# Turned attention weights in rows of 2304 bytes, turned behind the masks, with the values two steps later

## The chip, the cores and the metric

The kernel runs on one core of a Trainium2 chip. The metric is the device time of one execution in microseconds (us), the median of several runs. Engines are named as in the profile: PE is TensorE's matmuls (PEld its weight loads), DVE is VectorE, ACT is ScalarE, POOL is GpSimd, SP is SyncE, which here only issues DMAs; SPq, ACTq and so on are the sequencers of the engines.

## The reference

Attention with a threshold on 8 x 8 heads of 576 positions and 64 dimensions, then an MLP with a squared relu on the 4608 tokens that the heads give, all in float32.

```python
scores = scale * np.matmul(q, k.transpose(0, 1, 3, 2))
thresh = np.max(scores, axis=-1, keepdims=True) - tau
scores = np.where(scores >= thresh, scores, -1000000000.0)
attn = exp(scores - max);  attn = attn / (sum(attn) + 1e-09)
x = matmul(attn, v)            # (B,H,S,D) -> (B*S, H*D) = (4608, 512)
h = x @ w_in                   # 512 -> 2048
return np.maximum(h, 0.0) ** 2 @ w_out
```

## The kernel before, in words

**Visits and steps.** Two heads make a head pair. A visit is a head pair with some of its five blocks of queries (four of 128, and the odd one, number 4, of 64). The first twelve visits fill the time in which the weights of the MLP are read; from visit 12 on, visits come in pairs of two head pairs: the first visit of a pair (even number) has the odd block, shared by the two, and blocks 0 to 3; the second (odd number) has blocks 0 to 3. A step is one block of one visit, so a pair has nine steps: the odd block, four of the first visit, four of the second. `late_step` writes out what each of these steps puts on each engine, in program order; there is no scheduler behind it, and every engine does its work in that order.

**A step.** PE makes the scores (`scores_of_two` makes those of two blocks at once, in every second step). DVE takes the maxima (L303), ACT the exponents (L318), DVE applies the threshold, which the change's title calls masks (L330), and POOL divides by the sum (L340). The weights of a block then lie with queries on the partitions. For the product with the values they must have keys on the partitions: they have to be turned.

**Turning and placing.** In the visits from 11 on this is done in two moves. `turn_blocks` (L420) has DVE transpose blocks of 32 x 32 from `w` into `turned`, a buffer with two halves that are used in turn. `place_blocks` then moves these small blocks across partitions with DMAs from SP's queue into `wT` (L432 for blocks 0 to 3, L437 and L445 for the odd block): sixteen DMAs for a pair of blocks (four quarters of queries x four quarters of keys, 32 partitions each, 72 KB) and sixteen of half the size for an odd block. `turn_last(s)` issues the turning of the step before and whatever placing is due; when each placing is due stands in `place_at`. In the earlier visits PE turns the weights and ACT copies them (L381, L388, L393) into `wT`.

**The product with the values.** `mix` (L482) multiplies `wT` by the values when all blocks of a visit are placed. It makes two groups: one reads the columns ONE (blocks 0 and 1) and the odd block (LEFT or ODD), the other TWO (blocks 2 and 3). Within each the first sixteen or so matmul records are the eight terms of the four full key blocks; the last terms, for the odd keys, follow for both. It uses the PSUM banks of areas in which scores of even steps lie, so their masks have to be done first. `mixes` says in which step it stands: `lag` steps after the visit's last block; `at_end` puts it at the end of the step for first visits, else it stands near the start.

**The MLP** fills PE between these: `fill(quarter)` takes as many pieces (`mlp_in` L530, `unit` L638, `product` L744) from a queue as an even rate asks for. A piece's follow-ups on ACT, DVE and POOL (L646, L650, L569 and others) are issued one or two pieces later by `after()` and `some_later()`.

Of the kernel before, what the change touches and what calls it, by code (L numbers as in the profile page):

```python
# [19 lines left out]
def kernel(  # L20
# [52 lines left out]

    NC9 = 2 * NBLK + 1
    ODD, ONE, LEFT, TWO = 0, REST, REST + 2 * P, 2 * REST + 2 * P
    wT = const.tile([P, NC9, S + REST], FP32, name="wT")

    vs = [const.tile([P, 2 * NBLK + 2, D], FP32, name=f"vs{i}") for i in range(2)]
    qmid = const.tile([P, P], FP32, name="qmid")
# [291 lines left out]
    def turn(vis, i, part):  # L371

        w = weights[vis, i][0]
        ps = take("mm", (6, 7)) if early() and part == 1 else take("tx", (4, 5))
        ps = ps.rearrange("p (c n) -> p c n", n=P)
        if i < NBLK:
            cols = slice(i * P, (i + 1) * P)
            for n in range(3):
                c = 3 * part + n
                nc.tensor.transpose(ps[:, n, :], w.rearrange("p u k -> p (u k)")[:, c * P:(c + 1) * P], ident)  # L380
            nc.scalar.copy(wT[:, 3 * part:3 * part + 3, cols], ps[:, 0:3, :])  # L381
        elif part < 2:
            rows = slice(part * D, (part + 1) * D)
            for c in range(NBLK):
                at = part * REST + c * P
                nc.tensor.transpose(ps[:, c, 0:D], w[rows, 0, at:at + P], ident[rows, rows])
            at = part * (NBLK + 1)
            nc.scalar.copy(wT[:, at:at + NBLK, NBLK * P:S], ps[:, :, 0:D])  # L388
        else:

            for rows, keys in ((slice(0, D), slice(S - REST, S)), (slice(D, P), slice(0, REST))):
                nc.tensor.matmul(ps[rows, 0, 0:D], w[rows, 0, keys], ident[rows, rows], start=True, stop=True)
            nc.scalar.copy(wT[:, NBLK, NBLK * P:S], ps[:, 0, 0:D])  # L393

    blocks = {}

    def turn_blocks(vis, i):

        w = weights[vis, i][0]
        two = i < NBLK
        both = two or paired(vis)
        M = KB - 2
        if not two or i % 2 == 0:
            at = len(blocks) % 2 * NB
            size = 2 * KB * (1 + two) if both else KB + 2
            blocks[vis, i // 2] = turned[:, at:at + size * 32].rearrange("p (k u q) -> p k u q", u=1 + two, q=32)  # L410
        wb = blocks[vis, i // 2]
        if both:
            odd = M if i in (2, 3) else KB
            parts = [(0, 0, M, 0), (0, M, KB, 2 * M + 2 - odd), (1, M, KB, odd), (1, 0, M, KB + 2)]
            if odd == KB:
                parts[0:2] = [(0, 0, KB, 0)]
        else:
            parts = [(0, 0, KB, 2), (0, M, KB, 0)]
        for u, k0, k1, at in parts:
            nc.vector.transpose(wb[:, at:at + k1 - k0, i % 2, :],  # L420
                                w[:, u, k0 * 32:k1 * 32].rearrange("p (k q) -> p k q", q=32))

    def place_blocks(vis, pair, which=range(4)):

        wb = blocks[vis, pair]
        for qb in which:
            rows = slice(qb * 32, qb * 32 + 32)
            for j in range(4):
                to = wT[j * 32:j * 32 + 32, :, :]
                if pair < NBLK // 2:  # L430
                    at = (ONE, TWO)[pair] + qb * 64
                    nc.sync.dma_start(out=to[:, :, at:at + 64], in_=wb[rows, j::4, :, :].rearrange("p c u q -> p c (u q)"))  # L432
                    continue
                at = LEFT + qb % 2 * 32
                if paired(vis):
                    at = at if qb < 2 else ODD + qb % 2 * 32
                    nc.sync.dma_start(out=to[:, :, at:at + 32], in_=wb[rows, j::4, 0, :])  # L437
                else:


                    first = j if qb < 2 else KB + (j - KB) % 4
                    n = len(range(first, KB if qb < 2 else 2 * KB, 4))
                    c = first // 4
                    first += 2 if qb < 2 else -KB
                    nc.sync.dma_start(out=to[:, c:c + n, at:at + 32],  # L445
                                      in_=wb[rows, first:first + 4 * n - 3:4, 0, :])

    read_to = {"x": 0}

# [29 lines left out]
    def mix(n, cols):  # L479

        def term(ps, u, c, at, rows=slice(0, P), first=False, last=False):
            nc.tensor.matmul(ps[u * D:(u + 1) * D, :], vs[n % 2][rows, u * (NBLK + 1) + c, :],  # L482
                             wT[rows, NBLK if c == NBLK else u * (NBLK + 1) + c, at:at + ps.shape[1]],
                             start=first, stop=last)

        above, below = slice(0, D), slice(D, P)
        arrived(vs[n % 2])
        if not by_dma(n):
            ps = take("tx", (4, 5))[:, 0:cols.stop - cols.start]
            for c in range(NBLK):  # L490
                for u in range(2):
                    term(ps, u, c, cols.start, first=(c == 0))
            for u, rows in enumerate((above, below)):
                term(ps, u, NBLK, cols.start, rows, last=True)
            put(n, cols.start, ps, False)
            return
        n1, n2 = 2 * P + REST, 2 * P
        at = ODD if paired(n) and n % 2 else ONE
        one, two = bank[0], bank[4]
        groups = (one[:, 0:n1], at, (above, below)), (two[:, 0:n2], TWO, (below, above))  # L500
        for ps, x, _ in groups:
            for c in range(NBLK):
                for u in range(2):
                    term(ps, u, c, x, first=(c == 0))

        for ps, x, places in groups:
            for u, rows in enumerate(places):
                term(ps, u, NBLK, x, rows, last=True)
        put(n, 0, one[:, ONE - at:ONE - at + 2 * P], True)
        left = ODD if at == ODD else LEFT - at  # L510
        put(n, NBLK * P, one[:, left:left + REST], False)
        put(n, 2 * P, two[:, 0:n2], True)
# [282 lines left out]
    def paired(n):  # L795

        return n >= 3 * HP
# [17 lines left out]
    for s, (n, i) in enumerate(steps):  # L815

        if by_dma(n):
            mixed = {visits[n][1][-1]: (0, 3 if n % 2 else 2)}
        else:
            mixed = {x: (x, 3) for x in range(NBLK + 1)}  # L820
        if i in mixed:
            first, lag = mixed[i]
            cols = slice(first * P, S if by_dma(n) else min((i + 1) * P, S))
            mixes[s + lag] = (n, cols)
            g_ = visits[n][0]
            if g_ % HP == HP - 1:
                complete[s + lag] = g_ // HP * S + cols.stop
# [107 lines left out]
    for s, (n, i) in enumerate(steps):  # L935
# [3 lines left out]
        more = nxt < len(visits)  # L939
        if paired(n):  # L940

            a, b = (1, 2) if paired(n - 1) else (3, 3)
            place_at[s + a].append((n, 2, (0, 1)))
            place_at[s + b].append((n, 2, (2, 3)))
            place_at[s + 3].append((n, 0))
            place_at[s + 5].append((n, 1))
            place_at[s + 7].append((n + 1, 0))
            place_at[s + 9].append((n + 1, 1))
            prep_at[s].append(lambda n=n: prep_part(q, n))
            load_at[s].append(lambda n=n: load_part(q, n + 1))  # L950
            load_at[s + 2].append(lambda n=n: load_v(n))
            prep_at[s + 4].append(lambda n=n: prep_part(q, n + 1))
            load_at[s + 4].append(lambda n=n: load_v(n + 1))
        else:
            place_at[s + 3].append((n, 0))
            place_at[s + 4].append((n, 1))
            place_at[s + 5].append((n, 2))
# [34 lines left out]
    def late_step(s):  # L992
# [3 lines left out]
        if on:  # L996
            n, i = steps[s]
            if not odd:
                scores_of_two(s)
                turn_last(s)  # L1000
            maxima(s, [area(u, odd) for u in range(2)])
            after()
            some_later("gpsimd")
            exponents(n, i)
# [5 lines left out]
                for j in chunk_at.get(s, ()):  # L1010
                    add_chunk(j)

        at_end = s in mixes and (mixes[s][0] % 2 == 0 or not paired(mixes[s][0]))
        if not at_end:
            values()
        if odd or not on:
            turn_last(s)
        quarter = rate(s) / 4 if s < END else 1e9
        fill(quarter)
        some_later("vector")  # L1020
        some_later("gpsimd")
        smooth = at_end or s not in mixes
        if smooth:
            after()
        if on:
# [4 lines left out]
        if smooth:  # L1030
            fill(quarter)
            after()
            some_later("gpsimd")
        some_loads()
        some_later("vector")
        if not smooth:
# [2 lines left out]
        some_loads()  # L1039
        fill(quarter)  # L1040
        some_loads()
        if at_end:
            values()
        fill(quarter)
        some_loads()

# [144 lines left out]
```

## Time and profile before

| | us |
|---|---|
| time before, median of 3 runs | 1415.88 (1415.67 to 1416.69) |
| span of the profiled execution | 1411.2 |
| PE busy | 1326.5 (94%) |
| DVE, POOL, ACT busy | 952.6, 978.5, 581.3 |
| first placing DMA, last placing DMA issued | 243.9, 1248.4 |

A line of the page's groups reads: line, engine, operation, what it writes and reads, shapes, count | busy us, mean ns of one | idle time of the engine just before, and what ended most of it. A line of the waits reads: engine, tile and line that waited, what it waited for: us in total, times, the longest. In a timeline a line has start, length, engine, line, operation, and in brackets the idle time before it. PE's records are two to a float32 matmul.

### The profile page before, as it was taken

What the parts mean: (1) busy time and instruction counts of PE and PEld (TensorE: products, weight loads), DVE (VectorE), ACT (ScalarE), POOL (GpSimd) and SP (SyncE); (2) the same over time, 40 slices, a digit from 0 to 9 for tenths busy, and PEclk for the clock granted to TensorE, in tenths of its full rate; (3) what the DMA queues carried; (4) which work ended last, traced back from release to release, by engine and by line L of the source; (5) the groups of instructions that cost most, each with busy time, mean ns of one, the idle gap of its engine ahead of it and who ended that gap; (6) DMA issues with size and microseconds to landing.
All of it is one profiled execution on the core that took longest, in us unless ns stands there. A gap on an engine that the chain in (4) does not pass through costs nothing.

```text
span 1411.2 us, 25854 instructions
## 1 busy us (share of the span) xinstructions
PE 1326.5 (94%) x9112; PEld 1092.8 (77%) x9112; DVE 952.6 (68%) x2026; ACT 581.3 (41%) x1357; POOL 978.5 (69%) x1229
## 2 busy tenths in 40 slices
PE   7899999888979899999999999999999999999998
PEld 5676567667868787777888878787888777889997
DVE  6877776677757766676977687778877768622231
ACT  4777673214334343424352525252525243513322
POOL 3688774686776949577787788779786867552451
PEclk8999999989999999999999999999999999999999
DMA  7755431545554544554454546554655455420000
GB/s 152 160 151 139 125 71 36 86 78 103 97 107 83 115 86 88 95 103 90 87 117 84 111 81 117 95 99 91 109 102 102 83 107 92 92 49 1 16 16 16
DMA packets 406354, 128.15 MB, mean 91 GB/s; under 512 B 390064, under 2 KB 394448, under 8 KB 406224
## 3 DMA queue, kind: packets, MB, share of 16 engines
q1 hardware_dynamic: 385632, 95.10, 37.4%
q0 software_dynamic: 18288, 31.11, 8.3%
q8 instruction: 72, 1.18, 0.4%
q10 hardware_dynamic: 2304, 0.29, 0.2%
q14 instruction: 58, 0.48, 0.1%
HBM read 50.59 MB, written 9.44 MB: 43 GB/s over the span
## 4 chain that ended last, share of the span: by engine, by line
PE 62%; POOL 15%; DVE 7%; SPq 6%; issue 4%; ACT 4%; DMA 3%; ACTq 0%; DVEq 0%; POOLq 0%
PE big L638 19%; PE big L744 18%; PE big L482 9%; PE big L282 6%; SPq L432 4%; POOL w L340 3%; PE big L530 3%; PE big L266 3%; POOL g L569 3%; DVE w L330 2%; DMA wT<-turned 2%; PE big L709 2%; PE big L380 2%; DVE st L303 2%; DVE turned L420 1%
## 5 line engine op out<-in xcount | busy, mean ns | idle before, releaser
L303 DVE TENSOR_REDUCE st<-big 128x1 f32<-128x576 f32 x288 | 203.5, 745 | 121.0 <-PE big L282 87.1
L340 POOL TENSOR_SCALAR w<-w,st 128x576 f32<-128x576 f32 x269 | 235.9, 886 | 22.7 <-DVE st L333 15.2
L420 DVE STREAM_TRANSPOSE turned<-w 128x512 f32<-128x512 f32 (+2 forms) x388 | 176.5, 499 | 103.0 <-POOL w L340 88.3
L330 DVE SCALAR_TENSOR_TENSOR w<-big,st,w 128x576 f32<-128x576 f32 x269 | 208.2, 810 | 52.9 <-ACT w L318 52.7
L744 PE MATMUL big<-wo,gsum 128*128 128x256 f32 x1088 | 243.5, 381 | 0.0
L744 PEld LDWEIGHTS big<-wo,gsum 128*128 128x128 f32 x1088 | 204.7, 190 | 35.7 <-issue 8.0
L482 PE MATMUL big<-wT,vs 128*64 128x128 f32 (+7 forms) x1700 | 180.7, 371 | 35.5 <-DMA wT<-turned 13.0
L638 PE MATMUL big<-xT,w_in_sb 128*128 128x128 f32 x1536 | 191.3, 280 | 8.2 <-ACT g L663 5.1
L338 POOL TENSOR_SCALAR st<-st 128x2 f32<-128x2 f32 (+1 forms) x148 | 34.8, 235 | 234.4 <-DVE w L330 226.7
L638 PEld LDWEIGHTS big<-xT,w_in_sb 128*128 128x128 f32 x1536 | 182.3, 195 | 18.3 <-issue 8.1
L482 PEld LDWEIGHTS big<-wT,vs 128*64 128x64 f32 (+1 forms) x1700 | 101.2, 141 | 109.2 <-issue 47.1
L744 PE MATMUL big<-wo,g 128*128 128x256 f32 x816 | 184.3, 381 | 0.0
L318 ACT ACTIVATE w<-big,st 128x576 f32<-128x576 f32 x269 | 183.5, 733 | 0.0
L744 PEld LDWEIGHTS big<-wo,g 128*128 128x128 f32 x816 | 151.8, 190 | 22.7 <-issue 3.6
L315 ACT ACTIVATE st<-st 128x2 f32<-128x2 f32 (+1 forms) x148 | 30.3, 204 | 287.4 <-DVE st L303 286.4
L282 PE MATMUL big<-kT,qT 64*128 64x256 f32 (+3 forms) x768 | 114.1, 422 | 5.6 <-DVE qT L240 4.4
L650 DVE TENSOR_TENSOR g<-big,g 128x512 f32<-128x512 f32 x96 | 64.5, 677 | 69.4 <-PE big L638 64.4
L282 PEld LDWEIGHTS big<-kT,qT 64*128 64x128 f32 x768 | 87.4, 189 | 27.1 <-issue 8.5
L646 ACT ACTIVATE g<-g 128x512 f32<-128x512 f32 x96 | 60.3, 629 | 69.8 <-DVE g L650 69.6
L520 POOL TENSOR_TENSOR gsum<-g 128x512 f32<-128x512 f32 x34 | 44.5, 1310 | 60.2 <-ACT g L647 59.8
L647 ACT ACTIVATE g<-g 128x512 f32<-128x512 f32 x128 | 80.7, 630 | 4.1
L638 PE MATMUL big<-t,g 128*128 128x128 f32 x512 | 64.7, 283 | 7.2 <-POOL g L569 6.3
(114 smaller groups left out, 2141.2 us busy)
## 6 DMA issues: line engine op xcount, KB each, us to landing
wT<-turned SPq DMA_DIRECT2D x800, 72.0 KB, 2.2
wo<-in_moe_w_in_dram SPq DMA_DIRECT2D x16, 512.0 KB, 4.5
wo<-in_moe_w_out_dram SPq DMA_DIRECT2D x16, 512.0 KB, 3.7
out_dram<-osb POOLq DMA_DIRECT2D x32, 256.0 KB, 2.4
ql<-in_q_dram POOLq DMA_DIRECT2D x96, 72.0 KB, 3.0
wT<-turned SPq DMA_DIRECT2D x192, 36.0 KB, 2.1
kl<-in_k_dram POOLq DMA_DIRECT2D x88, 72.0 KB, 2.6
vs<-in_v_dram POOLq DMA_DIRECT2D x48, 128.0 KB, 3.3
```

Of the source, the lines that this page charges most:

```text
L282: nc.tensor.matmul(big[to, at + x0:at + x1], lhsT, keys[u * D:(u + 1) * D, x0:x1], start=True, stop=True)
L303: nc.vector.tensor_reduce(out=mx[:, u:u + 1], in_=sc[u], axis=AX.XY, op=ALU.max)
L318: nc.scalar.activation(out=w[:, u, :].rearrange("p (h k) -> p h k", h=2), in_=sc[u], func=AF.Exp, bias=bias[:, u:u + 1], scale=SCALE)
L330: nc.vector.scalar_tensor_tensor(out=wu, in0=sc[u], scalar=thr[:, u:u + 1], in1=wu, op0=ALU.is_ge, op1=ALU.mult, accum_out=sm[:, u:u + 1])
L340: nc.gpsimd.tensor_scalar(out=w[:, u, :], in0=w[:, u, :], scalar1=z[:, u:u + 1], scalar2=rcp[:, u:u + 1], op0=ALU.add, op1=ALU.mult)
L420: nc.vector.transpose(wb[:, at:at + k1 - k0, i % 2, :], w[:, u, k0 * 32:k1 * 32].rearrange("p (k q) -> p k q", q=32))
L482: nc.tensor.matmul(ps[u * D:(u + 1) * D, :], vs[n % 2][rows, u * (NBLK + 1) + c, :], wT[rows, NBLK if c == NBLK else u * (NBLK + 1) + c, a ...
L638: nc.tensor.matmul(to[:, f, :], factor(j, p, q, c)[:, f * P:(f + 1) * P], part[:, c, :], start=(p in "125" and f == 0 and c == 0), stop=(p ...
L646: nc.scalar.activation(out=to, in_=to if src is None else src, func=AF.Relu)
L647: nc.scalar.activation(out=to, in_=to, func=AF.Square)
L650: nc.vector.tensor_tensor(out=x, in0=to, in1=x, op=ALU.add)
L744: nc.tensor.matmul(to, left[:, f, :], wo[:, slot, f, :], start=(f == 0), stop=(f == HF - 1))
```

## The change

It has three parts, as its title says.

The layout of `wT` goes from [key chunk, query] to [group of 64 queries, key chunk, query in the group], and that of `turned` with it, so that what one placing DMA of a full pair of blocks moves in a partition is one run of 9 x 64 floats, 2304 bytes, on both sides; before it was nine runs of 256 bytes. The odd block's placing keeps its nine runs of 128 bytes. The readers of `wT` in `mix` take groups of 64 columns, each 2304 bytes after the other.

`turn_last`, with turning and placing, moves in `late_step` from behind the scores (even steps) or behind the values (odd steps) to behind the masks and the division of the step.

The values of a pair's first visit move from the end of the pair's seventh step (lag 2, `at_end`) to near the start of its ninth (lag 4); those of the second visit stay where they were, in the third step of the next pair. The placing of the second visit's first two blocks, which overwrites what the first visit's values read, moves from step 7 to step 8 (counted from 0).

```diff
-    wT = const.tile([P, NC9, S + REST], FP32, name="wT")
+    wT = const.tile([P, S // REST + 1, NC9, REST], FP32, name="wT")
...
-            blocks[vis, i // 2] = turned[:, at:at + size * 32].rearrange("p (k u q) -> p k u q", u=1 + two, q=32)
+            t = turned[:, at:at + NB]
+            blocks[vis, i // 2] = t.rearrange("p (j c u q) -> p c j u q", j=4, u=2, q=32) if two else t.rearrange("p (k q) -> p k q", q=32)
...
+            move(wb[:, 0:h, :, :], whole_[:, 0, :, :, :])
+            if i < 2:
+                move(wb[:, h, :, :].rearrange("p (u j) q -> p u j q", u=2), rest_[:, :, 0, :, :])
+            else:
+                move(wb[:, h, 2:4, :], rest_[:, 0, 0, :, :])
+                move(wb[:, h, 0:2, :], rest_[:, 1, 0, :, :])
+            move(wb[:, h + 1:, :, :], whole_[:, 1, :, :, :])
...
-                    at = (ONE, TWO)[pair] + qb * 64
-                    nc.sync.dma_start(out=to[:, :, at:at + 64], in_=wb[rows, j::4, :, :].rearrange("p c u q -> p c (u q)"))
+                    nc.sync.dma_start(out=to[:, (ONE, TWO)[pair] // REST + qb, :, :].rearrange("p c q -> p (c q)"),
+                                      in_=wb[rows, :, j, :, :].rearrange("p c u q -> p (c u q)"))
...
-                             wT[rows, NBLK if c == NBLK else u * (NBLK + 1) + c, at:at + ps.shape[1]],
+                             wT[rows, at // REST:(at + ps.shape[1]) // REST, NBLK if c == NBLK else u * (NBLK + 1) + c, :],
...
-            mixed = {visits[n][1][-1]: (0, 3 if n % 2 else 2)}
+            mixed = {visits[n][1][-1]: (0, 3 if n % 2 else 4)}
...
-            a, b = (1, 2) if paired(n - 1) else (3, 3)
+            a, b = (1, 2) if paired(n - 1) else (2, 2)
...
-            place_at[s + 7].append((n + 1, 0))
+            place_at[s + 8].append((n + 1, 0))
...
             if not odd:
                 scores_of_two(s)
-                turn_last(s)
...
-        at_end = s in mixes and (mixes[s][0] % 2 == 0 or not paired(mixes[s][0]))
-        if not at_end:
-            values()
-        if odd or not on:
-            turn_last(s)
+        values()
...
+        turn_last(s)
         some_loads()
...
-        if at_end:
-            values()
```

More of the change, by code (lines that the diff above doesn't have):

```diff
@@ L376, in turn @@
         if i < NBLK:
-            cols = slice(i * P, (i + 1) * P)
             for n in range(3):
@@ L380, in turn @@
                 nc.tensor.transpose(ps[:, n, :], w.rearrange("p u k -> p (u k)")[:, c * P:(c + 1) * P], ident)
-            nc.scalar.copy(wT[:, 3 * part:3 * part + 3, cols], ps[:, 0:3, :])
+            nc.scalar.copy(wT[:, 2 * i:2 * i + 2, 3 * part:3 * part + 3, :].rearrange("p g c q -> p c g q"),
+                           ps[:, 0:3, :].rearrange("p c (g q) -> p c g q", g=2))
         elif part < 2:
@@ L387, in turn @@
             at = part * (NBLK + 1)
-            nc.scalar.copy(wT[:, at:at + NBLK, NBLK * P:S], ps[:, :, 0:D])
+            nc.scalar.copy(wT[:, 2 * NBLK, at:at + NBLK, :], ps[:, :, 0:D])
         else:
@@ L392, in turn @@
                 nc.tensor.matmul(ps[rows, 0, 0:D], w[rows, 0, keys], ident[rows, rows], start=True, stop=True)
-            nc.scalar.copy(wT[:, NBLK, NBLK * P:S], ps[:, 0, 0:D])
+            nc.scalar.copy(wT[:, 2 * NBLK, NBLK, :], ps[:, 0, 0:D])
     blocks = {}
@@ L404, in turn_blocks @@
         two = i < NBLK
-        both = two or paired(vis)
         M = KB - 2
@@ L408, in turn_blocks @@
             at = len(blocks) % 2 * NB
-            size = 2 * KB * (1 + two) if both else KB + 2
-            blocks[vis, i // 2] = turned[:, at:at + size * 32].rearrange("p (k u q) -> p k u q", u=1 + two, q=32)
+            t = turned[:, at:at + NB]
+            blocks[vis, i // 2] = t.rearrange("p (j c u q) -> p c j u q", j=4, u=2, q=32) if two else t.rearrange("p (k q) -> p k q", q=32)
         wb = blocks[vis, i // 2]
[L412 to L418, printed above, removed]
+        move = nc.vector.transpose
+        if two:
+            wb = wb[:, :, :, i % 2, :]
+            whole_, rest_ = (w[:, :, x0 * 32:x1 * 32].rearrange("p u (c j q) -> p u c j q", q=32, j=n)
+                             for x0, x1, n in ((0, M, 4), (M, KB, 2)))
+            h = M // 4
+            move(wb[:, 0:h, :, :], whole_[:, 0, :, :, :])
[5 more added lines that the diff above has]
+            move(wb[:, h + 1:, :, :], whole_[:, 1, :, :, :])
+            return
+        parts = [(0, 0, KB, 0), (1, M, KB, KB), (1, 0, M, KB + 2)] if paired(vis) else [(0, 0, KB, 2), (0, M, KB, 0)]
         for u, k0, k1, at in parts:
-            nc.vector.transpose(wb[:, at:at + k1 - k0, i % 2, :],
-                                w[:, u, k0 * 32:k1 * 32].rearrange("p (k q) -> p k q", q=32))
+            move(wb[:, at:at + k1 - k0, :], w[:, u, k0 * 32:k1 * 32].rearrange("p (k q) -> p k q", q=32))
     def place_blocks(vis, pair, which=range(4)):
@@ L428, in place_blocks @@
             for j in range(4):
-                to = wT[j * 32:j * 32 + 32, :, :]
+                to = wT[j * 32:j * 32 + 32, :, :, :]
                 if pair < NBLK // 2:
-                    at = (ONE, TWO)[pair] + qb * 64
-                    nc.sync.dma_start(out=to[:, :, at:at + 64], in_=wb[rows, j::4, :, :].rearrange("p c u q -> p c (u q)"))
+                    nc.sync.dma_start(out=to[:, (ONE, TWO)[pair] // REST + qb, :, :].rearrange("p c q -> p (c q)"),
+                                      in_=wb[rows, :, j, :, :].rearrange("p c u q -> p (c u q)"))
                     continue
-                at = LEFT + qb % 2 * 32
+                at = slice(qb % 2 * 32, qb % 2 * 32 + 32)
                 if paired(vis):
-                    at = at if qb < 2 else ODD + qb % 2 * 32
-                    nc.sync.dma_start(out=to[:, :, at:at + 32], in_=wb[rows, j::4, 0, :])
+                    nc.sync.dma_start(out=to[:, (LEFT if qb < 2 else ODD) // REST, :, at], in_=wb[rows, j:2 * KB:4, :])
                 else:
@@ L444, in place_blocks @@
                     first += 2 if qb < 2 else -KB
-                    nc.sync.dma_start(out=to[:, c:c + n, at:at + 32],
-                                      in_=wb[rows, first:first + 4 * n - 3:4, 0, :])
+                    nc.sync.dma_start(out=to[:, LEFT // REST, c:c + n, at], in_=wb[rows, first:first + 4 * n - 3:4, :])
     read_to = {"x": 0}
@@ L1021, in late_step @@
         some_later("gpsimd")
-        smooth = at_end or s not in mixes
+        smooth = s not in mixes
         if smooth:
```

## The prediction, made blind

> **What bounds the kernel now.** I read the page first (busy shares, slices), then who waited for whom on TensorE (PE), then PE's timeline around each large gap, and last VectorE's (DVE's) timeline, to see what arrives late.
>
> ```profile
> PE 1326.5 (94%) x9112; PEld 1092.8 (77%) x9112; DVE 952.6 (68%) x2026; ACT 581.3 (41%) x1357; POOL 978.5 (69%) x1229
> L420 DVE STREAM_TRANSPOSE turned<-w 128x512 f32<-128x512 f32 (+2 forms) x388 | 176.5, 499 | 103.0 <-POOL w L340 88.3
> L482 PE MATMUL big<-wT,vs 128*64 128x128 f32 (+7 forms) x1700 | 180.7, 371 | 35.5 <-DMA wT<-turned 13.0
> wT<-turned SPq DMA_DIRECT2D x800, 72.0 KB, 2.2
> ```
>
> PE is the bound: 94% busy, no other engine above 69%. The change takes no matmul away, so it can win only idle time of PE and time at a reduced clock. The idle time is small: 1411 less 1326.5, 85 us, some 24 of them before 250 us, where hardly anything changes. What is left shows in PE's waits:
>
> ```profile
> PE big L482 <- DMA wT<-turned: 13.0, 4, 6.4
> PE big L482 <- DVE w L330: 6.3, 1, 6.3
> PE big L638 <- POOL g L569: 6.3, 9, 1.2
> PE big L482 <- DVE turned L420: 5.7, 1, 5.7
> PE big L638 <- ACT g L663: 5.1, 3, 2.8
> PE big L282 <- DVE qT L240: 4.4, 1, 4.4
> ```
>
> The largest belong to L482, the product with the values. PE's timeline at one of them, and the windows just before, in, and after that gap:
>
> ```profile
> 404.13 2.37 PE L482 MATMUL big<-wT,vs 128*64 128x320 f32 x16
> 412.86 4.33 PE L482 MATMUL big<-wT,vs 128*64 128x256 f32 x24 [6.36 <-DMA wT<-turned]
> ...
> 400.00:406.50 6.50, 6.50 (x54) 5.07 (x52) 5.00 (x11) 3.97 (x9) 6.28 (x9) 1.00 0.88 188
> 406.50:412.90 6.40, 0.04 (x4) 0.07 (x3) 5.07 (x13) 0.74 (x2) 6.22 (x11) 0.74 0.65 124
> 412.90:420.10 7.20, 7.20 (x48) 4.85 (x50) 0.09 (x1) 2.24 (x8) 1.86 (x3) 0.76 0.33 68
> ```
>
> The columns of a window are PE, PEld, DVE, ACT, POOL busy, then the clock, the DMA share, GB/s. The reader sees the first product of a visit (ONE) run, the second (TWO) stand for 6.4 us until the placing DMAs of the second pair land, and a clock of 0.76 after the gap. Reading the timeline at every such product of a pair's first visit gives gaps of 3.0, 6.3, 5.6, 2.4, 1.6 us (ends at 330.2, 412.8, 493.8, 575.8, 898.2) and two of 0.6: 20 us. Each ends 0.3 to 0.4 us after the last of sixteen placing DMAs lands. The product of visit 11, before the pairs begin, waits 6.3 us for DVE and 2.6 us for its last placing.
>
> [...] 0.74 and 0.76 above are half clock for part of a window, and gaps of 5 us and more have it. [...] The trace: this queue's 385,632 packets take 37.4% of 16 engines, 0.374 x 16 x 1411.2 / 385,632 = 21.9 ns each, and a placing DMA lands 2.2 us after issue. So larger rows should free the rings, and shorten the 2.2 us little. [...] L709 moves 512 columns in two separate runs, eight in 3.44 us, 430 ns or 0.84 ns a column; L744 with 256 contiguous ones takes 7.07 us for 32, 221 ns or 0.86.
>
> **The change part by part.**
>
> *Rows of 2304 bytes.* 800 of 1008 placing DMAs (16 a pair of blocks) go from 32x9 pieces of 256 bytes to 32 rows. What costs now is SyncE's issue: 612 ns each, back to back, so sixteen take 9.8 us, up to 11 us where the rings are crowded. The trace has no SBUF to SBUF issue with one run per partition. Its bounds are the weight loads with one run a partition (L134, medians 346 and 442 ns) and 612 ns (no gain; 128-byte and 256-byte pieces cost the same, so bytes and pieces don't set it). I take 450 ns, near the dearer of the two load rows: sixteen in 7.2 us, 2.6 us less. Landing 2.2 to about 2.1.
>
> *The transposes.* Blocks 0 and 1: 772+215+679 ns become 679+310+679 (310 is the 128-wide L244): no difference. Blocks 2, 3: the same four. ACT's copies to wT in the early part keep their size (479 ns). Scattered writes: taken at nothing, as the old ones were scattered in runs of 32 as well.
>
> *Turning behind masks.* Today DVE reaches a block's transposes before the next block's masks, and stands there for POOL's division: 88.3 us, 45 times. Behind the masks the division is long done. The maxima, masks and so POOL's division of the next block come up to 2 us earlier where that stop was on the way. The price: the turning itself comes later. In the trace at 919.98 (scores of the odd block) the turning ran 919.85 to 921.5. Now DVE first has maxima (to 922.2), masks (exponents to 924, masks to 925), qT (0.8) and a sum (0.4), then 1.6 us of turning: done near 927.9, about 6.4 us later. Queued behind the turning on DVE are only the next maxima, which wait for the next scores anyway; behind the later placing stand only placings.
>
> *First visit's product in the next one's third step.* It moves from the end of that visit's second step to the start of its fourth, some 14 us later; its placing comes 6 us later and is quicker. The margin, now -6 to +1 us, becomes positive by several: the 20 us go. No chunk of tokens completes with a first visit (only odd visits close a batch row), so no MLP work is held back.
>
> *Second visit's product* stays in place, but its placing starts 6.4 us later. Today it lands just ahead: at 935.3 for a product at 936.24, at 858.2 for 858.4. After: issue from 927.9 takes 7.2 us to 935.1, landed 937.2. The TWO terms that need it come 2.37 us after the product's start, 938.6: spare 1.4 us. Crowded ones will miss; I allow 0.6 us on average for twelve pairs, 7 us.
>
> *Visit 11.* Its 32 placings from 260.9 landed at 284.6. Sixteen at 450 ns end at 268.1, sixteen at 600 ns (other form, unchanged) at 277.7, landed 279.6: the product starts 5 us sooner, and its DVE wait shrinks with the masks first.
>
> *Sum.* First visits 20; visit 11 5; half clock: 0.05 x 315 us (clock 0.95 from 285 to 600 us), 0.01 x 320 and 0.43 x 12 (279 to 291) are 24 us of lost clock, of which I put 14 outside the gaps themselves, and 9 with the gaps removed; qT (4.4 us, once) half, 2; the L638 waits for factors and squares (6.3+5.1+4.7+4.2 = 20) a quarter, 5, as DVE and POOL run ahead. Less 7. 20+5+9+2+5-7 = 34: 1415.9 - 34 = 1382.
>
> **The rivals.**
>
> *B, the issue isn't the rows' doing.* It stays at 612 ns: the second visit's placing ends at 937.7, lands 939.9, 1.3 us after the TWO terms want it, 2 to 2.5 when crowded. 12 x 2 = 24 us in place of 7, and 2 us less at visit 11: gain 34 - 19 = 15, 1401. For: the issue time doesn't follow sizes today. Against: every row of one run per partition issues faster. [...]
>
> *C, slower.* Runs of 64 columns slow the moving reads of L482. A quarter more on its 155 us with 256 and 320 columns (62.8+54.6+20.4+17.6) is 39: 1382 + 39 = 1421. Against: L709. Four-dimensional transposes at twice the time would put 1.6 us ahead of each second visit's placing, 19 us in all, and add to it.
>
> *D, more comes loose.* Second visits always in time (7 more) and another half of the L638 waits (10): 51, 1365. For: DVE's 88 us of standing were shared out over every step. Against: POOL is 72 to 78% busy between 285 and 1260 us, and PE's stops are what let it catch up.
>
> **How the numbers follow.** Forecast 0.5, D 0.15, B 0.2, C 0.15. The range reaches from a little below D to B's far end, 1362 to 1412, leaving out C and little else. Faster: the forecast, D and three quarters of B, 0.80; within 0.2%: the rest of B, 0.05; slower: C, 0.15.
>
> **What would show it.** Right: no gap over 1 us ahead of a first visit's TWO terms; DVE's wait for POOL w at the transposes near nothing; placing issues near 450 ns; far fewer packets on the placing queue; PE busy time down by some 10 us with the clock, its idle time by 25. Wrong: issues still near 610 ns with L482 gaps at second visits (B); longer L482 matmuls or transposes (C); PE's waits for POOL's factors growing by what the values gave up.

## The result, and the profile after

The time after is 1402.86 us (1399.23 to 1404.88, 4 runs) against 1416.29 us; the ratio is 0.9899, 95% interval 0.9875 to 0.9923. The kernel is 13.4 us faster, where 34 were forecast. The page of after is that of the fastest of its four runs. Lines below are from the page of the kernel after; L437 is the placing of a full pair of blocks (L432 before), L486 the product with the values (L482 before), L642 the MLP's `unit` (L638 before), L573 the factor sums (L569 before).

```profile
PE 1316.7 (94%) x9112; PEld 1086.3 (78%) x9112; DVE 946.3 (68%) x2026; ACT 585.0 (42%) x1357; POOL 975.6 (70%) x1229
q1 hardware_dynamic: 180832, 95.10, 29.5%
L486 PE MATMUL big<-wT,vs 128*64 128x128 f32 (+7 forms) x1700 | 183.7, 375 | 45.3 <-DVE w L330 15.1
L417 DVE STREAM_TRANSPOSE turned<-w 128x512 f32<-128x512 f32 x100 | 68.8, 688 | 7.3 <-DMA wT<-turned 6.6
wT<-turned SPq DMA_DIRECT2D x800, 72.0 KB, 2.1
```

PE's busy time fell by 9.8 us, about as forecast. Its idle time fell by only 3.9 us (84.7 to 80.8), where 25 were forecast. The placing queue's packets are less than half (385,632 to 180,832), and the rings' share for the same bytes went from 37.4% to 29.5%. DVE no longer stands for POOL's division ahead of the transposes (88.3 us before). That did not leave DVE with more time: it now waits longer for PE's scores ahead of the maxima (L303) and for ACT's exponents ahead of the masks (L330). The first two lines are of before, the others of after:

```profile
L303 DVE TENSOR_REDUCE st<-big 128x1 f32<-128x576 f32 x288 | 203.5, 745 | 121.0 <-PE big L282 87.1
L330 DVE SCALAR_TENSOR_TENSOR w<-big,st,w 128x576 f32<-128x576 f32 x269 | 208.2, 810 | 52.9 <-ACT w L318 52.7
...
L303 DVE TENSOR_REDUCE st<-big 128x1 f32<-128x576 f32 x288 | 204.0, 747 | 149.1 <-PE big L282 114.9
L330 DVE SCALAR_TENSOR_TENSOR w<-big,st,w 128x576 f32<-128x576 f32 x269 | 208.9, 813 | 93.6 <-ACT w L318 93.4
```

And the idle time ahead of L486 rose from 35.5 to 45.3 us. PE's waits say who:

```profile
PE big L486 <- DVE w L330: 15.1, 5, 3.8
PE big L486 <- DMA wT<-turned: 10.5, 3, 4.7
PE big L486 <- DVE st L333: 8.0, 2, 4.7
PE big L642 <- POOL gsum L573: 4.7, 2, 3.3
PE big L642 <- POOL g L573: 3.5, 3, 2.0
```

The L642 waits halved (20.3 us in the four lines of before, here 4.7+3.5 and two small ones of 1.8 and 1.0). The L486 waits shown carry three names, two of them of DVE. PE's timeline at one such wait, with DVE's just before, shows that the names mislead:

```profile
423.18 1.20 PE L282 MATMUL big<-kT,qmid 64*64 64x384 f32 x16
...
438.93 2.37 PE L486 MATMUL big<-wT,vs 128*64 128x320 f32 x16
444.86 2.63 PE L486 MATMUL big<-wT,vs 128*64 128x256 f32 x24 [3.56 <-DVE st L332]
```

```profile
428.98 0.78 DVE L240 STREAM_TRANSPOSE qT<-ql 128x576 f32<-128x576 f32 x1
429.69 0.67 DVE L417 STREAM_TRANSPOSE turned<-w 128x512 f32<-128x512 f32 x1
430.28 0.20 DVE L421 STREAM_TRANSPOSE turned<-w 128x64 f32<-128x64 f32 x1
430.40 0.20 DVE L422 STREAM_TRANSPOSE turned<-w 128x64 f32<-128x64 f32 x1
430.53 0.67 DVE L423 STREAM_TRANSPOSE turned<-w 128x512 f32<-128x512 f32 x1
```

This is a second visit's product. The scores of the odd block start at 423.18, the last transposes of the visit end at 431.20, SP issues the sixteen DMAs from 431.26 to 441.47, the last lands at 444.42, and the TWO terms, wanted from 441.30, start at 444.86. Reading all of them: gaps over 0.25 us stand at the second visits' product in ten of the twelve pairs, 0.6 to 4.7 us, 29.6 us in sum, each ended 0.4 us after the last of its sixteen DMAs landed. At first visits one gap of 2.1 us is left of the 20.9 us of before (at 805.4, with no landing in the 4.6 us ahead of it: there the masks may well be what PE waits for).

### The profile page after: what moved, and what is told of

The parts are those of the page before. It is cut to its first block, busy times and chain, and to the rows that moved or that the text cites. A ratio compares the mean times of both kernels' runs of the same rounds, so it can differ in the third digit from the quotient of the medians.

```text
span 1397.5 us, 25994 instructions
## 1 busy us (share of the span) xinstructions
PE 1316.7 (94%) x9112; PEld 1086.3 (78%) x9112; DVE 946.3 (68%) x2026; ACT 585.0 (42%) x1357; POOL 975.6 (70%) x1229
## 3 DMA queue, kind: packets, MB, share of 16 engines
q1 hardware_dynamic: 180832, 95.10, 29.5%
q10 hardware_dynamic: 2304, 0.29, 0.2%
## 4 chain that ended last, share of the span: by engine, by line
PE 77%; DVE 8%; ACT 4%; POOL 4%; issue 3%; SPq 3%; DMA 1%; ACTq 0%; DVEq 0%; POOLq 0%
PE big L748 25%; PE big L642 25%; PE big L486 10%; PE big L282 8%; PE big L534 3%; PE big L266 3%; DVE w L330 3%; DVE st L303 2%; PE big L713 2%; PE big L379 2%; ACT w L318 2%; SPq L437 1%; ACT wT L380 1%; DMA wT<-turned 1%; DVE gsum L772 1%
## 5 line engine op out<-in xcount | busy, mean ns | idle before, releaser
L303 DVE TENSOR_REDUCE st<-big 128x1 f32<-128x576 f32 x288 | 204.0, 747 | 149.1 <-PE big L282 114.9
L330 DVE SCALAR_TENSOR_TENSOR w<-big,st,w 128x576 f32<-128x576 f32 x269 | 208.9, 813 | 93.6 <-ACT w L318 93.4
L340 POOL TENSOR_SCALAR w<-w,st 128x576 f32<-128x576 f32 x269 | 227.6, 856 | 22.7 <-DVE st L333 15.0
L486 PE MATMUL big<-wT,vs 128*64 128x128 f32 (+7 forms) x1700 | 183.7, 375 | 45.3 <-DVE w L330 15.1
L486 PEld LDWEIGHTS big<-wT,vs 128*64 128x64 f32 (+1 forms) x1700 | 102.6, 142 | 120.6 <-issue 32.3
L642 PE MATMUL big<-xT,w_in_sb 128*128 128x128 f32 x1536 | 187.2, 276 | 0.6 <-DVE g L654 0.6
L642 PEld LDWEIGHTS big<-xT,w_in_sb 128*128 128x128 f32 x1536 | 179.4, 192 | 8.0 <-issue 5.4
L315 ACT ACTIVATE st<-st 128x2 f32<-128x2 f32 (+1 forms) x148 | 30.5, 206 | 270.8 <-DVE st L303 269.7
L282 PE MATMUL big<-kT,qT 64*128 64x256 f32 (+3 forms) x768 | 106.8, 416 | 0.2
L282 PEld LDWEIGHTS big<-kT,qT 64*128 64x128 f32 x768 | 84.4, 186 | 14.5 <-issue 4.3
L524 POOL TENSOR_TENSOR gsum<-g 128x512 f32<-128x512 f32 x34 | 45.3, 1332 | 63.0 <-ACT g L651 62.7
L417 DVE STREAM_TRANSPOSE turned<-w 128x512 f32<-128x512 f32 x100 | 68.8, 688 | 7.3 <-DMA wT<-turned 6.6
L642 PE MATMUL big<-xT,gsum 128*128 128x128 f32 x512 | 63.7, 277 | 5.1 <-POOL gsum L573 4.7
```

Source lines behind the costliest of these rows:

```text
L282: nc.tensor.matmul(big[to, at + x0:at + x1], lhsT, keys[u * D:(u + 1) * D, x0:x1], start=True, stop=True)
L303: nc.vector.tensor_reduce(out=mx[:, u:u + 1], in_=sc[u], axis=AX.XY, op=ALU.max)
L330: nc.vector.scalar_tensor_tensor(out=wu, in0=sc[u], scalar=thr[:, u:u + 1], in1=wu, op0=ALU.is_ge, op1=ALU.mult, accum_out=sm[:, u:u + 1])
L340: nc.gpsimd.tensor_scalar(out=w[:, u, :], in0=w[:, u, :], scalar1=z[:, u:u + 1], scalar2=rcp[:, u:u + 1], op0=ALU.add, op1=ALU.mult)
L417: move(wb[:, 0:h, :, :], whole_[:, 0, :, :, :])
L642: nc.tensor.matmul(to[:, f, :], factor(j, p, q, c)[:, f * P:(f + 1) * P], part[:, c, :], start=(p in "125" and f == 0 and c == 0), stop=(p ...
```

## The experiments

All are compared with runs of the kernel before on the same chip. "Second visits' gaps" are sums of the idle time of PE just ahead of the product with the values in the paired visits, read off the brackets of the timeline (those over 0.15 us). The product is L486, or L482 in the kernels with pieces of 256 bytes. The kernel before took 1414.1 to 1416.3 us on the chips used, so small differences are read from the ratios. The theory under test: the gain of the first visits was given back at the second visits, whose placing now comes too late for its product ("late placing").

**The parts alone.** The rows without the new order:

```diff
-            mixed = {visits[n][1][-1]: (0, 3 if n % 2 else 4)}
+            mixed = {visits[n][1][-1]: (0, 3 if n % 2 else 2)}
...
-            a, b = (1, 2) if paired(n - 1) else (2, 2)
+            a, b = (1, 2) if paired(n - 1) else (3, 3)
...
-            place_at[s + 8].append((n + 1, 0))
+            place_at[s + 7].append((n + 1, 0))
... # and late_step as in the kernel before
```

> The layout alone: rows of 2304 bytes, but turning ahead of the masks and the values in the steps of before. Theory 'late placing' (the new wait is that the second visit's product waits for its placing, because sixteen issues still take 9.3 us and start 6 us later): here the placing starts as early as before and its sixteen issues end about 1 us sooner, so the first visits' gaps shrink from 20 to about 12 us, second visits have none, time about 1406. Rival 'the rows make the whole gain': about 1402, with the first visits' gaps near 5 us.

Measured: 1404.4 us, ratio 0.9936 (0.9921 to 0.9951). First visits' gaps are 15.6 us (3.1, 4.6, 4.4, 2.7, 0.8), second visits have none. The rows alone are worth 10 us. The time lies between the theory's 1406 and the rival's 1402; the gaps, forecast at 12 and 5, and none at second visits, speak for the theory. One of them:

```profile
410.13 4.24 PE L486 MATMUL big<-wT,vs 128*64 128x256 f32 x24 [4.59 <-DMA wT<-turned]
```

The order without the rows (the kernel before with `late_step`, lags and placing steps of after):

> The order alone: turning behind the masks and the values' steps of after, but pieces of 256 bytes. Theory 'late placing': first visits have no gap; sixteen issues take 9.8 to 10.7 us, so the gaps of second visits grow from 29 to about 40 us, time about 1414. Rival 'the rows make the whole gain and the order costs nothing': about 1416 with second visits' gaps as in after, near 29 us.

Measured: 1415.69 us, ratio 1.0015 (1.0005 to 1.0025). Second visits' gaps are 41.7 us. So the order alone gains nothing: it takes away the 20.9 us at first visits and half of the waits at the MLP's `unit`, and gives more back at second visits.

The values' steps alone, on the kernel before:

```diff
-            mixed = {visits[n][1][-1]: (0, 3 if n % 2 else 2)}
+            mixed = {visits[n][1][-1]: (0, 3 if n % 2 else 4)}
...
-            a, b = (1, 2) if paired(n - 1) else (3, 3)
+            a, b = (1, 2) if paired(n - 1) else (2, 2)
...
-            place_at[s + 7].append((n + 1, 0))
+            place_at[s + 8].append((n + 1, 0))
...
-        if at_end:
-            values()
```

> Before, with the values' steps of after alone: pieces of 256 bytes, turning first. Theory 'late placing': no gaps at first visits; the 32 placings between a first visit's product and the second's take 20 to 21 us in place of 19, so second visits' gaps are 12 us plus some 1.2 us for each of twelve pairs, about 27; time about 1404. Rival 'rows don't matter once the values are late': about 1390.

Measured: 1403.84 us, ratio 0.9928 (0.9912 to 0.9945), gaps in the pairs 24.2 us, all at second visits, where 27 were expected. As the theory has it.

**The turning.** After, with turning and placing back ahead of the masks, values and rows as in after:

```diff
                 scores_of_two(s)
+                turn_last(s)
...
+        if odd or not on:
+            turn_last(s)
...
-        turn_last(s)
```

> After, but turning and placing where they stood before (ahead of the masks), values as in after. Theory 'late placing': the second visit's last placing now starts when the placing of its first two blocks has been issued, about 6 us after the odd block's scores instead of 8, and lands at about 18.3 us, just when it is wanted: second visits' gaps fall from 29 to under 10 us; VectorE stands for POOL's division again (about 90 us in total), which gives PE back some 9 us of waits at L642; time about 1388. Rival 'masks first is what pays': about 1410.

Measured: 1390.27 us, ratio 0.9835 (0.982 to 0.9849). Second visits' gaps are 12.6 us. DVE stands again, and the L642 waits are back (22 us of idle time there):

```profile
DVE turned L417 <- POOL w L340: 72.5, 40, 5.0
```

So turning behind the masks, the part of the change meant to free DVE, costs some 9 us net by the ratios (0.9835 against 0.9899; the profiled spans, 1387.0 and 1397.5, give 10.5). Does it cost in every step, or in the one where the placing is short of time? After, with turning first in the odd block's step alone:

```diff
                 scores_of_two(s)
+                if i == NBLK:
+                    turn_last(s)
...
-        turn_last(s)
+        if not on or i != NBLK:
+            turn_last(s)
```

> After, but in the pair's first step alone (the odd block) turning and placing stand ahead of the masks; in the other eight steps behind them. Theory 'late placing': second visits' gaps as in the kernel with all turning first, about 12 us in place of 29; the L642 waits as in after, about 11 us in place of 22; so some 10 us below that kernel, 1380. Rival 'the L642 waits don't follow the place of the turning': 1390.

Measured: 1378.95 us, ratio 0.976 (0.9738 to 0.9783). The L642 idle time is 11 us, as in after, and second visits' gaps 17.5 us (12 were expected). The kernel beats both: the loss lay in one step of nine, and in the other eight the masks first pay. Its profile is of its slowest run, 1385.1 us, so 6 us of the gain of the median run are in no trace.

**Is it the issue of the placing?** SP's queue spends 589 ns (median) on each DMA of a full pair of blocks. After, with eight of the sixteen DMAs of the second visit's last two blocks left out:

```diff
-            place_at[s + 9].append((n + 1, 1))
+            place_at[s + 9].append((n + 1, 1, (0, 1)))
```

> After, with eight of the sixteen placing DMAs of the second visit's last two blocks left out (the second visits' product then reads stale weights in half of the columns TWO). It takes away 5 us of issuing and nothing else of the order. Theory 'late placing, bound by the issue on one queue': the placing lands some 16 us after the odd block's scores, two before it is wanted; second visits' gaps fall from 29 us to under 3, time about 1370. Rival 'the gaps come from the masks that the profile names as the releaser (DVE w L330)': gaps stay, about 1400.

Measured: 1363.43 us, ratio 0.9633 (0.9618 to 0.9647). The products of the pairs run through without a gap:

```profile
432.29 4.79 PE L486 MATMUL big<-wT,vs 128*64 128x320 f32 x40
...
964.60 4.79 PE L486 MATMUL big<-wT,vs 128*64 128x320 f32 x40
967.80 0.82 DVE L330 SCALAR_TENSOR_TENSOR w<-big,st,w 128x576 f32<-128x576 f32 x1 [1.14 <-ACT w L318]
```

The masks stand where they stood, and at 964.60 the TWO terms are under way before the masks that came last in after's gaps have even begun (967.80). So "DVE w L330" and "DVE st L333" in the waits of after were not what PE waited for at second visits: of several semaphores, DVE's events fell close to the landing (for after's product at 444.86: the last landing at 444.42, DVE's L332 from 444.53 to 444.69). The run also issues 96 DMAs fewer, so its 39 us below after are not all of the gaps: in the profiled runs PE is idle 27.8 us less and, at a higher clock (0.988 against 0.983), busy 8.0 us less. From visit 11 on its only L486 gaps are those of that visit. Its idle time at L642 is 15 us, 4 more than after's.

The same DMAs shared between two queues:

```diff
             for j in range(4):
+                queue = (nc.sync, nc.scalar)[j % 2]
...
-                    nc.sync.dma_start(
+                    queue.dma_start(
```

> After, with the placing DMAs issued in turn by SP and by ACT. Theory 'late placing, bound by the issue on one queue': sixteen issues take about 5 us, second visits' gaps vanish (29 us and about 5 us of half clock), time about 1372, somewhat more where ACT's squares wait behind an issue. [...]

Measured: 1601.51 us, ratio 1.1335 (1.1311 to 1.1359), where about 1372 was expected. The median DMA of this run still takes its queue some 600 ns (588 on SP, 602 on ACT), so two do run side by side, and the gaps at the pairs' products are gone. But ACT's own work stood behind its share of the issues:

```profile
ACT g L651 <- DMA wT<-turned: 134.5, 17, 11.1
ACT seen L295 <- DMA wT<-turned: 80.9, 11, 11.5
ACT st L315 <- DMA wT<-turned: 76.4, 9, 10.8
```

I had put ACT at 42% busy and so free. But its work stands in program order behind the issues: eight of them, with their waits for turned blocks and for earlier landings, hold the step that leads to the next exponents (L315) for up to 10.8 us.

**What an issue costs**, by itself:

```python
for x in range(16):   # and other forms, each in a loop of its own
    lo = x % 4 * 32
    nc.sync.dma_start(out=rows[lo:lo + 32, x, :], in_=src[0:32, 0:R])
```

> Only DMAs from SP's queue; attention and MLP are left out, and the output holds no result. Sixteen of 32 rows of 2304 bytes inside SBUF, ten of 32 x 9 pieces of 256 bytes, eight of 128 rows, eight of 64 rows, sixteen of 32 pieces of 256 bytes, eight loads of 32 rows and three of 128 rows from DRAM, eight stores of 32 rows. If the issue's cost is one of the instruction: 500 to 610 ns for all forms inside SBUF, whatever bytes and partitions, 330 to 440 for the loads. If it is one of the pieces: the 32 rows and the 32 short pieces well under the 32 x 9.

The instructions' durations (min/median/max, ns), with `rows` 32 x 2304 bytes, `pieces` 32 x 9 x 256, `short` 32 x 256, `full` 128 x 2304, `half` 64 x 2304, all inside SBUF; then the loads from DRAM (32 and 128 rows) and the stores to it:

```profile
L44 SPq DMA_DIRECT2D rows<-src x16: 582/589/605, 2.1 to 11.6; - x16
L47 SPq DMA_DIRECT2D pieces<-src x10: 610/612/677, 12.2 to 18.2; - x10
L55 SPq DMA_DIRECT2D short<-src x16: 588/589/679, 29.9 to 39.6; - x16
L49 SPq DMA_DIRECT2D full<-src x8: 599/612/725, 18.8 to 23.5; - x8
L52 SPq DMA_DIRECT2D half<-src x8: 596/678/721, 24.3 to 29.2; - x8
L58 SPq DMA_DIRECT2D loaded<-in_moe_w_in_dram x8: 394/420/577, 0.7 to 42.7; - x8
L60 SPq DMA_DIRECT2D loaded<-in_moe_w_in_dram x3: 422/430/431, 43.1 to 44.1; - x3
L62 SPq DMA_DIRECT2D out_dram<-src x8: 314/422/436, 44.5 to 48.2; - x8
```

One run a partition saves 23 ns of 612. Bytes hardly count: 8 KB and 288 KB differ by the same 23 ns. One form falls out: 64 rows take 678 ns, above the 500 to 610 that were expected of all forms inside SBUF, and dearer than 128; why isn't shown (their least is 596, and they were issued right behind the eight largest). What counts most in this run is where the two ends are: 420 to 430 ns with one end in DRAM, 589 to 678 with both in SBUF.

**More time for the second visit's placing.** Second visits' product two steps later as well:

```diff
-            mixed = {visits[n][1][-1]: (0, 3 if n % 2 else 4)}
+            mixed = {visits[n][1][-1]: (0, (5 if paired(n) else 3) if n % 2 else 4)}
...
-            a, b = (1, 2) if paired(n - 1) else (2, 2)
+            a, b = (1, 4) if paired(n - 1) else (2, 2)
... # ODD's placing ahead of the turning in that step, (n, 0) placed in step 4
```

> After, with the second visits' product two steps later too (the next pair's fifth step; the placings that overwrite what it reads move behind it; the MLP's tokens of a batch row come two steps later). Theory 'late placing': no gap over 0.5 us at a product of the pairs, 29 us and some 4 us of half clock less: about 1370. Rival 'PE's stops only move': L642 waits grow from 11 us to over 25, time over 1385.

Measured: 1405.36 us, ratio 0.9941 (0.9926 to 0.9956). The products of the pairs have no gap over 0.2 us, as expected; but PE's idle time at L642 is 32 us, and the rival's forecast (over 25 there, over 1385 us) is what came. The reason is a wait of my own making:

```profile
DVE turned L417 <- DMA wT<-turned: 64.3, 24, 8.6
```

The ODD half of the odd block now stays in its half of `turned` until that product, and the next visit's transposes want that half: DVE stands, and the MLP behind it. No run gives the odd block a buffer of its own, so what the later product alone would bring isn't shown.

The first visit's product a quarter of a step earlier, on the 1379 us kernel:

```diff
-            mixed = {visits[n][1][-1]: (0, 3 if n % 2 else 4)}
+            mixed = {visits[n][1][-1]: (0, 3)}
... # the first visit's values() and the placing of (n + 1, 0) after the third fill(quarter) of step 7
```

> After, with the odd block's step turning ahead of the masks (the 1379 us kernel), and the first visit's values, with the placing that waits for them, a quarter of a step earlier: in the eighth step behind its masks. Theory 'late placing': the chain product of the first visit, 32 issues, product of the second starts some 2 us sooner; second visits' gaps fall from 19 us to about 6, time about 1365. Rival 'the first visit's product now waits for its masks': gaps appear there instead, time 1375 to 1385.

Measured: 1403.22 us, ratio 0.9911 (0.9895 to 0.9928): the rival's mechanism, and more than its time. Second visits have no gap any more; first visits have one in each pair, 1.0 to 3.3 us and 28.3 us in sum, since the product needs the bank whose masks are only just being made:

```profile
486.26 2.21 PE L282 MATMUL big<-kT,qT 64*128 64x256 f32 x16
491.47 4.79 PE L486 MATMUL big<-wT,vs 128*64 128x320 f32 x40 [3.00 <-DVE w L330]
```

Here "DVE w L330" is named rightly: all forty records wait at once, not the TWO terms alone.

| kernel | us | ratio | gaps at the pairs' products, us |
|---|---|---|---|
| rows alone | 1404.4 | 0.9936 | 15.6, first visits |
| values' steps alone | 1403.8 | 0.9928 | 24.2 |
| values' steps and masks first | 1415.7 | 1.0015 | 41.7 |
| rows and values' steps | 1390.3 | 0.9835 | 12.6 |
| all three (after) | 1402.9 | 0.9899 | 31.7 |
| all three, odd block's step turning first | 1379.0 | 0.976 | 19.5 |

By the ratios the rows are worth 0.6% alone, 0.9% on top of the values' steps and 1.2% on top of values and masks (9 to 16 us); the values' steps 0.7% alone and 1.0% with the rows; masks first in every step costs 0.6 to 0.9%. No run has masks first with the values where they stood.

## Why the prediction was wrong, point by point

The direction was right; the size was off by more than half, and rival B (1401 us), given 0.2, is what happened. That B's number is so near is in part luck: its second visits lost 24 us where 29.6 were lost, its visit 11 won 3 where 1 was won, and the waits at qT and L642, which fell by some 7 us more than forecast, made up for it.

- *First visits, 20 us.* Right: 18.8 came. The move of the values did it: in the kernel with the values' steps alone they have no gap.
- *Second visits, 7 us.* This is the step that failed: 29.6 us. The turning ended 8.0 us after the odd block's scores, as forecast (7.9). The sixteen issues were put at 450 ns, 7.2 us; they took 10.2 us at 431.26: 589 ns each (median), and some 45 ns from the end of one to the start of the next, which the sum left out (10.0 us in the quietest sets). The 450 ns came from loads out of DRAM, the nearest row there was; the issue test has that kind at 420 to 430 ns and this one at 589. The rest is smaller: the last landing came 2.95 us after the end of the last issue, not 2.1 (the profile's 2.1 counts from the start of an issue, and on that count it was 3.5), and the product started 15.75 us after the scores, not 16.3. A spare 1.4 us became 3.6 us short. I also left out that in this step the placing before it, which waits for the first visit's product, keeps the queue until 429.6: even with turning first in this step (1390 us and 1379 us kernels) 12.6 and 17.5 us of gaps stay at second visits.
- *Visit 11, 5 us.* About 1: its gaps went from 8.9 to 7.8 us, for the same reason: its first sixteen issues took 10.8 us, not 7.2, and its placings landed at 283.7, not 279.6.
- *Half clock, 9 us.* Mean clock 0.979 to 0.983, 29.8 to 23.9 us of lost clock: 6, of which part is this run's own (after's four runs range from 0.978 to 0.983, and the profiled one is at the top). The reading that gaps of 5 us and more have half clock was too narrow: in before, gaps of 3.1 us (at 330.2) and 2.4 us (at 575.8) were followed by it too. In the traces of before and after, every half-clock stretch after 280 us starts on one grid of 3.41 us, and whether one comes goes with how much of the window ahead of it PE is idle. In the windows of after below this list, a gap of 2.39 us lies inside one window (PE busy 1.02 us) and the next one runs at half clock; the gap of 3.56 us at 444.86 is split by two windows (1.65 and 1.62 us busy) and no half clock follows. From 280 to 1330 us, the two traces together have 13 full-clock windows with 2.03 us or more idle, and half clock followed each; of the six with 1.76 to 2.00 us idle it followed one; those with 1.66 us and less had none.
- *qT, 2 us; L642, 5 us.* Better than forecast: 4 and 10. The masks first did the latter: the kernels with turning first all have 19 to 24 us of idle time at L642, those with masks first 10 to 11 (after, the order alone, and the odd step's variant); where the products' gaps are gone or moved it is 15 to 17 (half the placing, the first visit's product earlier).
- *Moving reads in runs of 64 columns and four-dimensional transposes, nothing.* Right. L486 with 320 columns is 451 ns before and after (the 256-column form, which holds the TWO terms that wait, 416 and 431), the 512-wide transposes 688 and 669 against 679.
- *Landing.* 2.2 to 2.1 us, as forecast. The rings did get freer: the queue lost 204,800 packets, all of them of the placing inside SBUF (800 x 32 x 8), and its packets' time fell by a fifth for the same bytes (37.4% to 29.5%).

The windows of the half clock (columns as in the prediction's: length; PE, PEld, DVE, ACT, POOL busy; clock, DMA share, GB/s):

```profile
750.27:753.68 3.41, 1.02 (x12) 0.86 (x12) 1.89 (x6) 1.36 (x3) 3.41 (x5) 1.00 0.46 98
753.68:757.09 3.41, 3.41 (x20) 1.45 (x17) 1.50 (x3) 0.33 (x2) 3.39 (x6) 0.50 0.75 137
...
439.65:443.07 3.42, 1.65 (x14) 0.59 (x10) 3.42 (x7) 1.67 (x4) 3.42 (x6) 1.00 0.64 158
443.07:446.48 3.41, 1.62 (x16) 1.26 (x16) 3.10 (x9) 0.00 (x0) 3.39 (x5) 1.00 0.69 101
446.48:449.89 3.41, 3.41 (x23) 2.40 (x20) 0.15 (x1) 0.83 (x4) 3.22 (x6) 1.00 0.29 43
```

So the change holds two parts that gain about as much (rows and values), and one that gains at L642 but delays, in one step of nine, the placing whose landing in before had 1.4 to 6.4 us to spare. The rows don't gain by a cheap issue, as was forecast: sixteen issues take 10.5 us on average with the rows alone, against 11.0, and 0.4 us of this is the shorter issue itself (23 ns each). How much of the gain comes from this, and how much from less crowded rings, isn't shown.

## What to carry to other kernels

A margin that the profile shows as "no wait" can be 1.4 us wide (in before, a last landing at 450.6 for TWO terms due at 452.1): before moving work behind other work, list every later consumer and read how long before its need it lands today. A cost that bounds the forecast is to be taken from a row with the same two ends, not the same shape (in the issue test, 32 rows and 72 KB take 589 ns inside SBUF and 420 ns out of DRAM). And the last releaser of a wait on several semaphores is a guess when events lie 0.3 us apart (444.42 and 444.69 above); leaving out half of the suspected work tells it.

## What the runs showed of the hardware that was not expected

In the issue test a DMA issued by SP took its queue 589 to 612 ns (medians) with both ends in SBUF and 420 to 430 ns with one end in DRAM. Inside SBUF, 8 KB took 589 ns and 288 KB 612, one run a partition 589 and nine 612, 32 partitions 589 and 128 612 (64 took 678). Moving half of the placing's issues to ACT's queue made the kernel 13% slower (1601.51 us), though in after ACT was busy 42% of the time. In after, a gap of PE of 2.39 us inside one 3.41 us window was followed by half clock in the next, and one of 3.56 us split over two by none.
